# Last dense block of an attention and two-layer expert kernel: low parts on VectorE, a constant subtracted on ScalarE, the element chain on 1024 columns, splits one half-step sooner

## The chip, the cores and the metric

One core of one Trainium2 chip. The metric is the device time of one execution in microseconds; lower is better. A core has a matmul engine (TensorE, PE in the rows, with its weight loads as PEld), VectorE (DVE), ScalarE (ACT), GpSimd (POOL) and SyncE, whose queue (SPq) starts the transfers. Each engine takes its instructions in the order in which the program gives them and waits on semaphores for the others.

## What is computed

Three blocks follow one another on 2304 tokens (4 sequences of 576): attention with 8 heads, a layer of 8 experts of which each token uses one, and a last dense block. The change concerns the last block alone:

```python
def _moe2_ref(x, w_in, w_out):        # x 2304 x 512, w_in 512 x 2048, w_out 2048 x 512
    h = x @ w_in
    g = h * np.cos(h)
    return (g @ w_out).astype(np.float32)
```

All tensors are float32. The kernel multiplies in a reduced form of float32 (fp32r): it splits each operand in a high part (a copy into fp32r) and a low part (operand minus high part), and adds three products, high x high, high x low and low x high.

## The kernel before

Attention and experts take the first 546 us; the function `moe2` (line 1384) is the last block and takes the rest, together with transfers and splits that run ahead of it.

**Units.** The 2304 tokens are a first group of 256 (g = 0) and four groups of 512 (g = 1 to 4). The 2048 hidden features are 8 pieces q of 256. The weights of half of them fit, so there are two passes, w = 0 (q = 0 to 3) and w = 1 (q = 4 to 7). The order of the units (lines 1400 to 1406) is g = 0 with four q, then g = 1 to 4 for w = 0, then g = 1 to 4 for w = 1, then g = 0 again. For g > 0 a piece q is a pair of units, i = 0 and i = 1, each a half-step; for g = 0 it is one unit. That makes 72 units; a group of 512 tokens is eight of them, and the groups begin at t = 4, 12, 20, 28, 36, 44, 52, 60.

**Layer 1** (`layer1`, line 1444) forms h for a piece of 256 features and 512 tokens by Strassen's method in seven products of half size (`product`, line 1437): i = 0 computes four (24 matmuls of 256 columns), i = 1 three (18). The factors are sums of quarters of x (`sums`, line 1418: four 512-column operations per group) and of w_in (`Seven.sums`, line 1347), each split in high and low part: seven tiles X0 to X6 (line 1395, one buffer each, so that a group overwrites those of the one before) and seven blocks per q in a slot. `middle` (line 1470) adds the products up: for i = 0 a copy p on ScalarE and four sums of 256 columns on VectorE, which also give half of the second h; for i = 1 two sums (512 and 256 columns) that finish both h.

**The element chain** of a unit, on 128 x 512: `angles` (line 1490) computes k = h / 2 pi + MAGIC on ScalarE, which rounds to a whole number; `reduced` (line 1494) calls `reduce` (line 1325): subtract MAGIC from k, and two scalar_tensor_tensor that take the multiple of 2 pi off h, all on VectorE; `sines` (line 1498) does Sin and Square on ScalarE; `cosines` (line 1503) one scalar_tensor_tensor on VectorE that gives g = -h cos(h) / 2; `split_g` (line 1507) the high part on ScalarE and the low part on GpSimd.

**Layer 2** (`layer2`, line 1514) adds g times w_out into four accumulators in PSUM, 12 matmuls of 512 columns per unit; after a group's last unit `results` (line 1543) takes them out and stores them: in pass 0 as partial sums to the scratch tensor Y1, in pass 1 added to what `recall` (line 1538) has read back.

**The order** is the loop at line 1598. In iteration t: layer 1 of unit t, chain steps of earlier units, `middle` of t, `split_g`, the work that falls due (`later.step`), layer 2 of unit t - 5. The helper `lag` gives the units of a chain step: for g > 0 it is one iteration later than for g = 0. Work that falls due: at t - 3 of a group's first unit `fetch` reads its x into the two buffers xd (shared with results and recall, so a fetch waits until a group's results are stored), at t - 2 `sums` runs on GpSimd, and the x splits (`split_x`, line 1432: high part ScalarE, low part VectorE) come two at t - 2, two at t - 1 and three at t.

**Weights.** `build` (line 1570) puts the seven-product weights of a piece q into a slot: `Seven.parts` (line 1376) loads, then high parts on ScalarE, sums on GpSimd and low parts on the engine given. Pieces 1 to 3 are built in iterations 0 to 9, pieces 4 to 7 from t1 - 14 to t1 + 3, where t1 = 36. `split_out` (line 1564) does the w_out pieces 4 to 7 at t1 - 1, + 1, + 3, + 5: high part on ScalarE, low part on GpSimd (`Dense.split`, line 803).

## Time and profile before

| | us |
|---|---|
| median of three runs | 1031.33 |
| lowest and highest | 1028.74, 1035.77 |
| the profiled execution | 1032.09 |
| its span, first to last instruction | 1030.3 |

In that span TensorE is busy for 930.1 us, VectorE 856.7, ScalarE 575.6, GpSimd 378.0. The mean granted TensorE clock is 0.958 of full speed. Times in the rows are microseconds from the span's start, unless marked ns. A row of the timeline gives start, duration, engine, line, operation, and output <- inputs with their shape; an idle time before it and what ended that stand in brackets. Tiles go by the names in the program: x are the split factors of layer 1, xt their sums, xd what was read or is to be stored, k and r the chain's tiles, ph the PSUM tile of layer 1, py that of layer 2, s and w weights, xc and xo raw weights.

### The profile page before, as it was taken

What the parts mean: (1) busy time and instruction counts of PE and PEld (TensorE: products, weight loads), DVE (VectorE), ACT (ScalarE), POOL (GpSimd) and SP (SyncE); (2) the same over time, 40 slices, a digit from 0 to 9 for tenths busy, and PEclk for the clock granted to TensorE, in tenths of its full rate; (3) what the DMA queues carried; (4) which work ended last, traced back from release to release, by engine and by line L of the source; (5) the groups of instructions that cost most, each with busy time, mean ns of one, the idle gap of its engine ahead of it and who ended that gap; (6) DMA issues with size and microseconds to landing.
All of it is one profiled execution on the core that took longest, in us unless ns stands there. A gap on an engine that the chain in (4) does not pass through costs nothing.

```text
span 1030.3 us, 20277 instructions
## 1 busy us (share of the span) xinstructions
PE 930.1 (90%) x7529; PEld 778.7 (76%) x7530; DVE 856.7 (83%) x1661; ACT 575.6 (56%) x1146; POOL 378.0 (37%) x433
## 2 busy tenths in 40 slices
PE   8999999999989999999996797989795879798996
PEld 4566666666669899898996686878685668687995
DVE  8958888888765678977988898898999998979872
ACT  8867777777774433434445554555564554544551
POOL 0034545455560122233224352435256442424231
PEclk9989999999999999999999799989898999998999
DMA  7965355545374645477763110303031122211202
GB/s 218 292 214 161 128 186 178 194 149 168 113 248 148 202 161 178 119 256 261 262 206 108 42 62 1 102 1 103 1 124 52 68 65 64 76 62 65 83 1 86
DMA packets 69161, 134.12 MB, mean 130 GB/s; under 512 B 7048, under 2 KB 19100, under 8 KB 69052
## 3 DMA queue, kind: packets, MB, share of 16 engines
q1 hardware_dynamic: 68764, 132.57, 39.7%
q8 instruction: 61, 1.00, 0.4%
q14 instruction: 48, 0.39, 0.1%
q10 hardware_dynamic: 288, 0.16, 0.1%
HBM read 94.38 MB, written 38.32 MB: 129 GB/s over the span
## 4 chain that ended last, share of the span: by engine, by line
PE 42%; DVE 27%; issue 6%; DMA 3%; POOL 1%; ACT 1%; SPq 0%; DVEq 0%; POOLq 0%; ACTq 0%
PE py L1528 11%; PE ph L1441 8%; PE pl L861 7%; PE po L880 6%; DVE x L1435 5%; DVE g L1505 3%; DVE r L1328 3%; PE pa L602 3%; DVE k L1327 3%; PE ps_s L524 3%; DVE h L1476 2%; DVE u L1476 2%; PE Tp L560 1%; DVE w L811 1%; DMA Wo<-f32a 1%
## 5 line engine op out<-in xcount | busy, mean ns | idle before, releaser
L1511 POOL TENSOR_TENSOR gl<-g,gh 128x512 fp32r<-128x512 f32 x72 | 101.4, 1409 | 265.6 <-ACT gh L1510 255.1
L1528 PE MATMUL py<-w,gh 128*128 128x512 f32 x576 | 188.9, 410 | 3.7 <-DVE xd L1553 2.6
L1441 PE MATMUL ph<-x,s 128*128 128x256 f32 x840 | 122.0, 300 | 58.2 <-DVE x L1435 46.1
L1441 PEld LDWEIGHTS ph<-x,s 128*128 128x128 f32 x840 | 115.1, 205 | 67.1 <-DVE x L1435 51.1
L1322 ACT ACTIVATE k<-h,magic 128x512 f32<-128x512 f32 x64 | 46.0, 719 | 150.4 <-DVE h L1476 150.4
L1528 PEld LDWEIGHTS py<-w,gh 128*128 128x128 f32 x576 | 108.6, 198 | 26.2 <-DVE xd L1553 3.4
L861 PE MATMUL pl<-xh,w 128*128 128x288 f32 x512 | 118.2, 306 | 0.5 <-DVE hl L866 0.5
L1528 PE MATMUL py<-w,gl 128*128 128x512 f32 x288 | 117.2, 407 | 1.1 <-POOL gl L1511 1.1
L534 DVE CUSTOM_DVE_ANT_0 s<-ps_s,Bp 128x576 f32<-128x576 f32 x112 | 81.1, 755 | 40.7 <-PE ps_s L524 31.1
L545 ACT ACTIVATE e<-s,mn 128x576 f32<-128x576 f32 x144 | 110.3, 769 | 6.8 <-DVE mn L534 6.6
L880 PE MATMUL po<-hh,w 128*128 128x288 f32 x512 | 112.8, 297 | 0.2 <-DVE w L811 0.2
L720 POOL TENSOR_TENSOR f32a<-f32a,raw 128x256 f32<-128x256 f32 x64 | 48.2, 753 | 146.6 <-DVE raw L718 118.2
L861 PEld LDWEIGHTS pl<-xh,w 128*128 128x128 f32 x512 | 88.4, 194 | 5.4 <-issue 3.2
L524 PEld LDWEIGHTS ps_s<-HL 64*128 64x128 f32 x768 | 57.3, 189 | 39.8 <-DVE mn L534 20.9
L524 PE MATMUL ps_s<-HL 64*128 64x288 f32 x768 | 76.6, 316 | 11.4 <-DVE mn L534 9.9
L880 PEld LDWEIGHTS po<-hh,w 128*128 128x128 f32 x512 | 86.3, 190 | 0.4 <-DVE w L811 0.4
L865 ACT ACTIVATE hh<-pl 128x288 fp32r<-128x288 f32 x64 | 26.3, 411 | 97.3 <-PE pl L861 96.1
L602 PE MATMUL pa<-eT,V 128*64 128x320 f32 (+1 forms) x512 | 79.4, 420 | 0.0
L861 PE MATMUL pl<-xl,w 128*128 128x288 f32 x256 | 77.4, 302 | 1.7 <-DVE xl L835 1.7
L880 PE MATMUL po<-hl,w 128*128 128x288 f32 x256 | 75.9, 297 | 0.0
L571 ACT ACTIVATE eT<-Tp 128x512 f32<-128x512 f32 x80 | 46.1, 598 | 41.3 <-PE Tp L560 41.2
L1528 PEld LDWEIGHTS py<-w,gl 128*128 128x128 f32 x288 | 56.4, 196 | 15.8 <-POOL gl L1511 1.9
(258 smaller groups left out, 2176.8 us busy)
## 6 DMA issues: line engine op xcount, KB each, us to landing
Bp<-in_w SPq DMA_DIRECT2D x38, 512.0 KB, 6.0
Bd<-ev SPq DMA_DIRECT2D x36, 295.5 KB, 3.7
Rqk<-in_qk SPq DMA_DIRECT2D x16, 576.0 KB, 5.3
raw<-in_w_in SPq DMA_DIRECT2D x32, 256.0 KB, 4.0
raw<-in_w_out SPq DMA_DIRECT2D x32, 256.0 KB, 3.7
xd<-X SPq DMA_DIRECT2D x16, 512.0 KB, 4.2
Bp<-Bd SPq DMA_DIRECT2D x28, 288.0 KB, 5.9
X<-xT SPq DMA_DIRECT2D x7, 1152.0 KB, 5.4
```

Of the source, the lines that this page charges most:

```text
L524: nc.tensor.matmul(p[:, hf, :HF], w, y, start=(x == 0), stop=(x == 2))
L534: nc.vector.tensor_tensor_reduce(out=h2(s), in0=ps[:, :, :HF], in1=h2(bias(hp, i)), scale=-0.125, scalar=3e38, op0=ALU.add, op1=ALU.min, a ...
L545: nc.scalar.activation(out=e[:, par, :], in_=s, func=AF.Exp, bias=mn, scale=-1.0, accum_out=acc)
L571: nc.scalar.activation(out=dst, in_=Tp[qh], func=AF.Copy)
L602: nc.tensor.matmul(pa[64 * par:64 * par + 64, :W], d["V"][:, k, par, :], x, start=(k == 0), stop=(k == 4))
L720: self.tc.nc.gpsimd.tensor_tensor(out=af[:], in0=af[:], in1=low, op=ALU.add)
L861: nc.tensor.matmul(ps[:, :HF], w[:, c, :], x[:, c, :], start=(n == 0), stop=(n == 3 * NP_ - 1))
L880: nc.tensor.matmul(self.acc[d][:, :HF], w[:, ds_], x, start=(f == 0 and n == 0), stop=(f == self.FC - 1 and n == 2))
L1435: eng.tensor_tensor(out=X[k][:, 1], in0=src, in1=X[k][:, 0].bitcast(F32), op=ALU.subtract)
L1441: nc.tensor.matmul(out, W[:, l, a, c, :], x[:, m, c, :], start=(first and n == 0), stop=(last and n == 5))
L1511: nc.gpsimd.tensor_tensor(out=lo, in0=g, in1=hi.bitcast(F32), op=ALU.subtract)
L1528: nc.tensor.matmul(st["acc"][k], x[:, c], a, start=(first and n == 0), stop=(last and n == (2 if g else 5)))
```

## The change

The chain of a pair of units (g > 0) runs once on 1024 columns, in tiles that `wide` hands out: one tile for the pair, of which g = 0 units use a half each. `lag` now gives the second unit of a pair without the extra iteration, and the chain steps of that pair all run then. MAGIC is taken off k by a second ScalarE instruction with a bias tile `back`; `reduced` keeps the two scalar_tensor_tensor. The cosine writes r in place. The low part of g is computed on VectorE, `split_g` runs at a lag of two, layer 2 at t - 4, and the loop ends one iteration sooner. The low parts of the seven-product weights go to GpSimd; of the four w_out pieces 4 and 6 have their low parts on VectorE, 5 and 7 on GpSimd. The first group's x splits are due one iteration sooner for the first five. The buffers of p and u fall to one each; k has one of 1024 columns, h, r, gh and gl two.

```diff
@@ -1388,12 +1388,20 @@
     later = Later()
     with ExitStack() as ctx:
         pool = lambda name, bufs, **kw: ctx.enter_context(tc.tile_pool(name=name, bufs=bufs, reuse_waits="tile", **kw))
-        wp, xp, tp, gp, dp = pool("p3w", 1), pool("p3x", 1), pool("p3t", 3), pool("p3g", 3), pool("p3d", 2)
+        wp, xp, tp, gp, dp = pool("p3w", 1), pool("p3x", 1), pool("p3t", 1), pool("p3g", 2), pool("p3d", 2)
         ps_h, ps_o = pool("ps_h", 4, space=PSUM), pool("ps_y", 1, space=PSUM)
         slots = dense.slots + [dense.slot(wp, "s1"), dense.seven(dense.blocks[1]), dense.seven(dense.blocks[0]),
                                dense.slot(wp, "s4")]
         X = [xp.tile([128, 2, 2, XG], F32R, name=f"x{k}") for k in range(7)]
-        t512 = lambda name, bufs=3: tp.tile([128, TG], F32, name=name, bufs=bufs)
+        pairs = {}
+
+        def wide(t, name, bufs, pool=tp, dt=F32):
+            w, g, q, i = units[t]
+            if g or q % 2 == 0:
+                pairs[name] = pool.tile([128, 2 * TG], dt, name=name, bufs=bufs)
+            return pairs[name] if g else pairs[name][:, TG * (q % 2):TG * (q % 2) + TG]
+
+        t512 = lambda name: tp.tile([128, TG], F32, name=name, bufs=1)
         xd = lambda name="xd", bufs=2: dp.tile([128, 1024], F32, name=name, bufs=bufs)
         v = nc.vector
 
@@ -1475,25 +1483,29 @@
             near, far = slice(0, XG), slice(XG, TG)
             add = lambda out, a, b: v.tensor_tensor(out=out, in0=a, in1=b, op=ALU.add)
             if i == 0:
-                p, u = st["p"], st["u"] = t512("p", 2), t512("u", 2)
-                h1 = d[t + 1]["h"] = t512("h", 4)
+                p, u = st["p"], st["u"] = t512("p"), t512("u")
+                hh = d[t + 1]["h"] = wide(t, "h", 2)
+                h0, h1 = st["h"] = hh[:, 0:TG], hh[:, TG:2 * TG]
                 nc.scalar.activation(out=p, in_=A, func=AF.Copy)
                 add(u[:, near], C[:, near], p[:, near])
                 add(u[:, far], C[:, far], u[:, near])
                 add(h1[:, far], u[:, far], p[:, far])
                 add(p[:, far], u[:, near], p[:, far])
             else:
-                h0 = d[t - 1]["h"] = t512("h", 4)
+                h0, h1 = st["h"]
                 add(h0, A, st["p"])
-                add(d[t]["h"][:, near], C[:, near], st["u"][:, far])
+                add(h1[:, near], C[:, near], st["u"][:, far])
 
         def angles(t):
-            k = d[t]["k"] = t512("k", 2)
+            k = d[t]["k"] = wide(t, "k", 1)
             turns(nc, k, d[t]["h"], bias)
+            nc.scalar.activation(out=k, in_=k, func=AF.Identity, bias=back)
 
         def reduced(t):
-            r = d[t]["r"] = t512("r", 3)
-            reduce(nc, r, d[t]["k"], d[t]["h"])
+            r, k = wide(t, "r", 2), d[t]["k"]
+            d[t]["r"] = r
+            v.scalar_tensor_tensor(out=r, in0=k, scalar=-PI2A, in1=d[t]["h"], op0=ALU.mult, op1=ALU.add)
+            v.scalar_tensor_tensor(out=r, in0=k, scalar=-PI2B, in1=r, op0=ALU.mult, op1=ALU.add)
 
         def sines(t):
             r = d[t]["r"]
@@ -1501,15 +1513,17 @@
             nc.scalar.activation(out=r, in_=r, func=AF.Square)
 
         def cosines(t):
-            g = d[t]["g"] = t512("g", 2)
-            v.scalar_tensor_tensor(out=g, in0=d[t]["r"], scalar=0.5, in1=d[t]["h"], op0=ALU.subtract, op1=ALU.mult)
+            r = d[t]["r"]
+            v.scalar_tensor_tensor(out=r, in0=r, scalar=0.5, in1=d[t]["h"], op0=ALU.subtract, op1=ALU.mult)
 
         def split_g(t):
-            g = d[t]["g"]
-            hi, lo = gp.tile([128, TG], F32R, name="gh"), gp.tile([128, TG], F32R, name="gl")
+            g = d[t]["r"]
+            n = 2 if units[t][1] else 1
+            hi, lo = (wide(t, x, 2, gp, F32R) for x in ("gh", "gl"))
             nc.scalar.activation(out=hi, in_=g, func=AF.Copy)
-            nc.gpsimd.tensor_tensor(out=lo, in0=g, in1=hi.bitcast(F32), op=ALU.subtract)
-            d[t] = dict(hi=hi, lo=lo)
+            v.tensor_tensor(out=lo, in0=g, in1=hi.bitcast(F32), op=ALU.subtract)
+            for i in range(n):
+                d[t + 1 - n + i] = dict(zip(("hi", "lo"), (x[:, TG * i:TG * i + TG] for x in (hi, lo))))
 
         def layer2(t):
             w, g, q, i = units[t]
@@ -1563,7 +1577,7 @@
 
         def split_out(q):
             dense.w[1, q] = dense.w[1, q - 4]
-            dense.split(B, 1, q, None, nc.gpsimd)
+            dense.split(B, 1, q, None, nc.gpsimd if q % 2 else v)
             if q < 7:
                 load_out(q + 1)
 
@@ -1571,13 +1585,15 @@
             for dt, fn in seven.parts(q, slots[k], eng):
                 at(t + dt, fn)
 
-        warm = t512("p", 2)
+        warm = t512("p")
+        back = tp.tile([128, 1], F32, name="back")
+        nc.gpsimd.memset(back, -MAGIC)
         nc.scalar.activation(out=warm[0:1, 0:1], in_=bias[0:1, :], func=AF.Sin, scale=0.0)
         fetch(0, 1)
         for k, t in enumerate((0, 3, 5)):
-            build(t, k + 1, k + 1, v)
+            build(t, k + 1, k + 1, nc.gpsimd)
         at(0, lambda: sums(v))
-        for t, k in ((1, 0), (1, 3), (2, 4), (2, 5), (3, 1), (3, 2), (4, 6)):
+        for t, k in ((0, 0), (0, 3), (1, 4), (1, 5), (2, 1), (3, 2), (4, 6)):
             at(t, lambda k=k: split_x(k, v))
         for (w, g), t in start.items():
             if g and (w, g) != (0, 1):
@@ -1593,22 +1609,23 @@
         for q in range(4, 8):
             seven.corner[q] = tiles[q // 6].rearrange("p c t -> p (c t)")[:, 512 * (q % 2):512 * (q % 2) + 512].rearrange(
                 "p (l c f) -> p l c f", l=2, c=2)
-            build(t1 - 14 + (0, 7, 10, 13)[q - 4], q, (4, 0, 1, 2)[q - 4], v)
+            build(t1 - 14 + (0, 7, 10, 13)[q - 4], q, (4, 0, 1, 2)[q - 4], nc.gpsimd)
             at(t1 - 1 + 2 * (q - 4), lambda q=q: split_out(q))
-        for t in range(N + 5):
+        for t in range(N + 4):
             if t < N:
                 layer1(t)
-            lag = lambda n: [s for s in (t - n, t - n - 1) if 0 <= s < N and (s == t - n) == (units[s][1] == 0)]
+            lag = lambda n: [s for s in (t - n, t - n) if 0 <= s < N and units[s][1] == 0][:1] + [
+                s for s in (t - n,) if 0 <= s < N and units[s][3] == 1]
             for work, n in ((angles, 1), (sines, 2), (reduced, 1), (cosines, 2)):
                 for s in lag(n):
                     work(s)
             if t < N:
                 middle(t)
-            for s in lag(3):
+            for s in lag(2):
                 split_g(s)
             later.step()
-            if t >= 5:
-                layer2(t - 5)
+            if t >= 4:
+                layer2(t - 4)
 
 
 MAGIC = 12582912.0
```

## Rows read from the trace of the kernel before

**Rows 1.** Windows: stretch and length, busy us per engine (instructions), granted clock, DMA share, GB/s

```profile
557.90:566.86 8.96, 0.12 (x3) 0.03 (x1) 8.64 (x13) 6.10 (x12) 3.81 (x4) 0.72 0.03 13
566.86:619.78 52.92, 44.56 (x252) 39.65 (x253) 48.75 (x68) 28.89 (x49) 23.64 (x20) 0.89 0.16 50
619.78:670.32 50.54, 44.66 (x266) 39.35 (x264) 44.25 (x66) 25.88 (x45) 17.13 (x13) 0.97 0.15 53
670.32:720.04 49.72, 45.76 (x266) 40.24 (x264) 45.29 (x68) 27.43 (x48) 19.75 (x17) 0.93 0.17 54
720.04:772.00 51.96, 45.30 (x266) 39.96 (x264) 50.01 (x71) 29.16 (x53) 22.88 (x17) 0.93 0.20 62
772.00:834.00 62.00, 46.51 (x259) 39.51 (x260) 60.58 (x74) 30.55 (x52) 34.75 (x24) 0.89 0.20 68
834.00:886.19 52.19, 45.85 (x270) 40.31 (x269) 47.68 (x70) 27.22 (x48) 20.53 (x15) 0.97 0.20 65
886.19:936.50 50.31, 44.59 (x265) 39.37 (x264) 44.29 (x68) 24.77 (x43) 17.16 (x13) 0.97 0.18 62
936.50:985.45 48.95, 45.70 (x267) 40.46 (x266) 43.89 (x73) 24.17 (x42) 12.23 (x9) 0.93 0.19 63
```

**Rows 2.** Chain that ended last, 936 us to the end: start, us, what

```profile
953.85 2.84 PE ph L1441 x24
956.69 2.80 PE py L1528 x12
959.49 2.12 PE ph L1441 x18
...
1005.41 16.81 PE py L1528 x72
```

**Rows 3.** Waits, 560 us to the end: us in total, times, longest us

```profile
PE ph L1441 <- DVE x L1435: 46.1, 19, 9.3
```

**Rows 4.** Timeline of all engines around 881 us

```profile
881.32 1.36 POOL L1422 TENSOR_TENSOR xt<-xd,xt 128x512 f32<-128x512 f32 x1
881.45 1.79 DVE L1435 TENSOR_TENSOR x<-xd,x 128x512 fp32r<-128x512 f32 x1
```

**Rows 5.** Single operations by line or tile: shortest/median/longest ns, first and last start

```profile
L1435 DVE TENSOR_TENSOR x<-xt,x x32: 676/684/1789, 563.6 to 949.3; 128x512 fp32r<-128x512 f32 x32
...
L1476 DVE TENSOR_TENSOR h<-ph,p x32: 677/684/687, 581.7 to 983.1; 128x512 f32<-128x512 f32 x32
...
L1476 DVE TENSOR_TENSOR h<-u,p x32: 424/425/614, 577.5 to 978.9; 128x256 f32<-128x256 f32 x32
...
L1327 DVE TENSOR_SCALAR k<-k x72: 411/426/2642, 559.7 to 1006.2; 128x512 f32<-128x512 f32 x72
...
L811 POOL TENSOR_TENSOR w<-xo,w x4: 2382/2684/3384, 778.5 to 821.2; 128x1024 fp32r<-128x1024 f32 x4
...
L1350 POOL TENSOR_TENSOR xc<-xc x32: 720/942/1195, 538.0 to 799.2; 128x256 f32<-128x256 f32 x32
```

**Rows 6.** Groups by form, 700 to 1000 us: busy us, mean ns, idle before

```profile
L1322 ACT ACTIVATE k<-h,magic 128x512 f32<-128x512 f32 x45 | 32.4, 719 | 109.2 <-DVE h L1476 109.2
...
L1500 ACT ACTIVATE r<-r 128x512 f32<-128x512 f32 x47 | 29.1, 620 | 0.0
...
L809 ACT ACTIVATE w<-xo 128x1024 fp32r<-128x1024 f32 x4 | 4.2, 1046 | 0.0
...
L1374 DVE TENSOR_TENSOR w<-xc,w 128x1024 fp32r<-128x1024 f32 x1 | 1.2, 1218 | 0.0
```

**Rows 7.** Timeline of SyncE's queue, 868 to 900 us

```profile
871.17 1.57 SPq L1557 DMA_DIRECT2D out<-xd  x2
874.01 1.84 SPq L1415 DMA_DIRECT2D xd<-X  x2
```

**Rows 8.** Timelines of VectorE and of GpSimd, 795 to 800 us

```profile
797.55 1.11 DVE L1329 SCALAR_TENSOR_TENSOR r<-k,r 128x512 f32<-128x512 f32 x1
...
796.06 4.36 POOL L1350 TENSOR_TENSOR xc<-xc 128x256 f32<-128x256 f32 x4
```

## The prediction, made before the changed kernel was run

> **What bounds the kernel now.** I cut the last stage (the second dense block, from 557.9 us to the end) at the first matmul of each group of 512 tokens and read the windows of those stretches first [rows 1]. A group asks the same matmuls everywhere, yet takes 49.0 to 62.0 us. The chain of waits says what an undisturbed pair of half-steps costs TensorE: 2.84 + 2.80 + 2.12 + 2.80 = 10.56 us, so 42.2 for the four pairs of a group [rows 2]. Every group is 7 to 20 us above that floor, and in each window it is VectorE that is busy for 44 to 61 us. In the waits the largest that TensorE suffers there is for the low parts of x, 46.1 us in 19 waits [rows 3]: the transition from one group to the next, where X is overwritten in place.
>
> Why VectorE is late there is seen in a timeline [rows 4]: the x split takes 1.79 us while GpSimd runs its 512-column sums, where the same operation at best takes 0.68 [rows 5]. GpSimd's own operation ends first, then the split runs. Operations that read PSUM escape: the 512-column sum h from ph is 677 to 687 ns in all 32 cases [rows 5], while the tensor_scalar on k goes from 411 to 2642 ns [rows 5]. So work on GpSimd is paid for on VectorE, about 1.1 us for each 512-column operation that collides.
>
> **The change, part by part.** Durations for 1024 columns: a VectorE tensor_tensor of that size takes 1.22 us and a ScalarE copy 1.05, against 0.68 and 0.62 for 512 [rows 5, 6]. The trace shows no 1024-column scalar_tensor_tensor, Sin, Square or biased Identity. Above, they are bounded by two halves (1.37 on VectorE, 1.24 on ScalarE, 1.44 with bias); below by the 1.22 and 1.05. I take the lower ones, which are of the same size, and for the biased form 0.72 + 0.43 = 1.15, the 0.43 being 1.05 - 0.62 [rows 6].
>
> *Low parts of g from GpSimd to VectorE.* Per group, eight GpSimd operations go that could each block VectorE by 1.1 us (8.8 at most); four of 1.22 come onto VectorE. The subtraction leaves VectorE (8 of 0.41 at best), and two pairs of three-operand instructions become single ones (12 fewer starts: 24 of 0.68 become 12 of 1.22, less 1.7 us). VectorE's own load: -3.3 - 1.7 + 4.9, about zero. What goes is the blocking.
>
> *The chain as a loop.* A pair's turn needs its h, which stands on VectorE behind the cosine of the pair before. From turn to turn: 1.15 turn + 1.15 subtraction + 2 x 1.22 + 1.05 + 1.05 + 1.22 cosine + 1.1 for the two h (0.68 + 0.42) = 9.2, with 0.1 for handing over 9.3 us. The four sums of the next pair (0.42 each [rows 5]) lie beside Sin and Square, gl beside the next turn. TensorE's 10.56 covers the loop with 1.3 to spare, 5.2 in a group. Against this stand, per group: two x splits ahead of a cosine +0.65 (0.6 each from start to start, of which 0.55 lie in its wait for Square), two x high parts ahead of a turn +1.05, three x splits +1.3 (1.8 less 0.5), results (2 on each engine or 4 on VectorE, about 0.6 each, 1.1 of it in the shadow of the next turn) +1.2, together 4.2; and the four GpSimd sums, 4 x 1.1 x 0.8 (VectorE is waiting for something the rest of the time) = 3.5. 7.7 - 5.2 = 2.5 over the floor: 44.7, taken as 45.0 a group. With two halves in place of each wide instruction the loop is 2 x 1.44 + 2 x 1.37 + 2 x 1.24 + 1.37 + 1.1 + 0.1 = 10.7, no spare, and a group is 42.2 + 7.7 = 50, as now; without collisions it is 43.
>
> *Split one half-step sooner.* Layer 2 runs four half-steps behind layer 1 instead of five. The y stores, and the fetch of the next X that follows them on SP (871.2 then 874.0 [rows 7]), move some 5 us ahead of the layer-1 work that they serve. With gl gone, GpSimd has nothing queued before the sums, so most of them end before the x splits begin. That is why I let the stall shrink to 2.5. The queues passed: SP's order of stores, recall and fetch is kept; ScalarE's high part waits for its cosine with the turn of the next pair behind it, 1.05 that is inside the loop's shadow of the two h. The tail after the last layer-1 step is now 72 layer-2 matmuls in 16.81 us [rows 2], six half-steps; one less is 2.8. This one fills TensorE's idle time at the stage's start instead.
>
> *Weight lows to GpSimd.* Per q of the seven-product weights: 512 + 256 (+256) + 1024 columns; a 1024-column low takes 2.38 there at best against 1.22 [rows 5], the 256-column sums that were there already 0.72 at best [rows 5]. GpSimd's load per q: 4 x 0.95 [rows 5] + 1.3 [rows 4] + 2 x 0.75 + 2.4 = 9.0 us. The matmuls that need them come two to three half-steps (10 us or more) after the last low is queued, so GpSimd's 2.4 to 3.4 is covered; late, it would cost TensorE up to 3 a q. What they cost VectorE: a 256-column sum lengthens the colliding 512-column operation from 0.68 to 1.11, so 0.43 [rows 5, 8], a 512-column one 1.1, the 1024 about 2.2 (2.62 against 0.41 is the longest k [rows 5]). Per q 1.7 + 1.9 + 2.2 = 5.8; three q and two of the four w_out lows (2.2 each) fall into the fourth and fifth group: 22 x 0.6 = 13, plus 2.4 for the two lows that VectorE takes, plus 2 x 2.5 as above: 20 over a floor of 84.4, so 105 instead of 52.0 + 62.0. Bounds 92 (no collision) and 114 (nothing gained). The third group has q = 4 in it: 47.
>
> The Trainium skill (SBUF — State Buffer, Who interferes with whom) has the loser fully blocked for the whole instruction. The long GpSimd operations agree, the 256-column ones show 0.43 [rows 5, 8] and not their 0.72; by the rule four sums cost 1.2 us more per q, and the pair of groups would be 107. I go by the row.
>
> The Trainium skill (ScalarE: Activation LUTs, Rules for kernel authors) would leave an add on VectorE. At best VectorE's is 0.41 against 0.72 for the biased form on ScalarE [rows 5, 6]; by the rule the loop would be about 0.3 shorter per pair and a group up to 1.2 us faster without this edit. But that operation averages more than its best because it is one that collides, up to 2.6 us [rows 5].
>
> *Start.* From 557.9 to 619.8 it is 9.0 + 52.9 = 61.9 us, 19.5 above a floor. VectorE loses the k operations and three sets of lows, GpSimd gains these. Between 0 and 8 gained; I take 4, mostly the layer-2 half-step that fits into the wait.
>
> **Sum.** Four ordinary groups (50.5, 52.2, 50.3, 49.0 = 202.0) to 180: -22.0. Third group 49.7 to 47: -2.7. Fourth and fifth 114.0 to 105: -9.0. Start -4.0, tail -2.8. Together -40.5. The profiled execution has 1032.1 us (span 1030.3): 991.6. It stands 0.8 above the median of 1031.3, so 991.
>
> **Rivals.**
> *TensorE-bound throughout.* For it: once past a transition, groups run at the floor today [rows 2]. Against: X is still overwritten in place. Groups 43, third 43, pair 88, start 55, tail 2.8: -30 - 7 - 26 - 7 - 3 = -73, 959.
> *Little left of it.* Wide instructions cost near two halves, or the builds collide fully: groups 48, third 49.7, pair 114, start -2, tail -2.8: -10 - 5 = -15, 1016. For it: VectorE's own load does not fall. Against: the 1.22 and 1.05 of the 1024-column rows.
> *Slower: the chain one pair deep.* Today's two half-steps interleave; now a pair goes through two ScalarE and VectorE turns with single k, p and u tiles. If the next pair's four sums, which wait for layer 1 and stand ahead of the cosine, fall into the loop rather than beside Sin and Square, it is 9.3 + 1.75 = 11.05 a pair, a group 44.2 + 7.7 = 51.9, on eight groups 1.7 more each against 50.2, less the tail: +11, and with the pair of groups no better 1043. It decides from a loop of 10.7, where a group equals today's. Against: GpSimd no longer blocks those sums.
>
> **Chances.** Forecast 0.63 (977 to 1006), TensorE-bound 0.15, little left 0.17, slower 0.05. Range 972 to 1013: it leaves out most of the first rival and the upper third of the second and third. About 1% (10 us) is what a measurement tells here. Faster by more: 0.63 + 0.15 + 0.12 = 0.90; within: 0.05 + 0.01 = 0.06; slower: 0.04.
>
> **What would show it.** Right: ordinary groups of 44 to 46 us between first layer-1 matmuls; TensorE's wait for x splits under 20 us in total; x splits near 0.68; first GpSimd sum of a transition at least 3 us ahead of the first x split; 60 matmuls in the last chain piece. Wrong: wide scalar_tensor_tensor above 1.3 us, VectorE's cosine waiting for GpSimd in ordinary groups, TensorE waiting for gl or for weight lows on GpSimd, or a loop from turn to turn above 10.7.

## The result and the profile after

The changed kernel takes 997.12 us (median of four runs, 996.5 to 998.38) against 1031.46 for the kernel before beside it; the ratio is 0.967, with a 95% interval of 0.963 to 0.970. The change gains 34 us; 40 were forecast (991, range 972 to 1013). The profiled execution of after has a span of 994.7 us, 35.6 less than before, and a mean clock of 0.973 of full speed against 0.958.

The windows of after, cut at the same matmuls as [rows 1] (stretch and length, busy us of PE, PEld, DVE, ACT and POOL with instructions, granted clock, DMA share, GB/s):

```profile
555.28:618.53 63.25, 45.98 (x265) 40.41 (x265) 54.82 (x62) 38.95 (x55) 33.97 (x25) 0.89 0.14 44
618.53:664.44 45.91, 42.73 (x265) 38.09 (x264) 38.59 (x50) 28.38 (x33) 11.24 (x8) 1.00 0.17 58
664.44:712.46 48.02, 44.22 (x265) 39.61 (x264) 38.78 (x49) 30.57 (x37) 16.85 (x11) 0.96 0.17 56
712.46:760.88 48.42, 44.65 (x265) 39.41 (x264) 41.29 (x51) 31.49 (x40) 21.05 (x15) 0.96 0.19 66
760.88:815.87 54.99, 46.59 (x265) 40.82 (x264) 43.99 (x50) 35.08 (x42) 27.50 (x18) 0.94 0.24 77
815.87:865.72 49.85, 45.35 (x266) 40.32 (x265) 43.72 (x58) 29.31 (x34) 7.74 (x6) 0.93 0.22 74
865.72:909.68 43.96, 42.21 (x265) 38.01 (x264) 38.96 (x52) 28.13 (x33) 7.53 (x4) 1.00 0.23 73
909.68:953.31 43.63, 42.37 (x267) 38.16 (x266) 35.69 (x50) 27.82 (x30) 0.00 (x0) 1.00 0.19 61
953.31:994.70 41.39, 33.27 (x193) 29.07 (x191) 19.69 (x26) 15.86 (x24) 0.00 (x0) 0.93 0.16 53
```

Read the second column against [rows 1]. The first row is the start of the stage, two rows of before (61.9 us); then come the seven other groups and the tail. Two groups now stand 1.8 and 1.4 us above the floor of 42.2, at a granted clock of 1.00. Term by term:

| stretch | before | forecast | after |
|---|---|---|---|
| start | 61.9 | 57.9 | 63.25 |
| four ordinary groups | 202.0 | 180 | 183.35 (45.91, 49.85, 43.96, 43.63) |
| third group | 49.7 | 47 | 48.0 |
| fourth and fifth (builds) | 114.0 | 105 | 103.4 |
| last stretch | 44.85 | 42.05 | 41.4 |
| the part that was not changed | 557.9 | 557.9 | 555.3 |

The last row is not put down to the edits: in the twelve profiles of after and its variants this part ended anywhere between 555.3 and 559.4 us, and the profile of after has the shortest. So 2.6 of the 35.6 us by which its span is shorter are not the change's. Each stretch is read from one profile, and stretches of the same code differ by a few us between profiles: the group of 49.85 us takes 47.1 in a variant below that changes the first three builds alone.

The waits of after, 560 us to the end (engine line waited for: us in total, times, longest):

```profile
PE ph L1449 <- DVE x L1443: 19.4, 15, 2.8
...
PE ph L1449 <- DVE r L1517: 12.5, 2, 10.8
...
PE ph L1449 <- ACT x L1442: 9.8, 6, 2.4
```

The wait for the low parts of x, 46.1 us in 19 waits before [rows 3], is 19.4 in 15, the longest 2.8 instead of 9.3. A new one has come: 9.8 us for the high parts of x on ScalarE, which has no row among TensorE's waits before. The 12.5 us for r is the start: TensorE waits there for the first cosine. Forms of the wide instructions (busy us, mean ns, idle before), then the shortest, median and longest of single operations:

```profile
L1322 ACT ACTIVATE k<-h,magic 128x1024 f32<-128x1024 f32 x32 | 36.5, 1142 | 4.8 <-DVE h L1484 4.6
...
L1502 ACT ACTIVATE k<-k,back 128x1024 f32<-128x1024 f32 x32 | 36.9, 1152 | 1.0
```

```profile
L1507 DVE SCALAR_TENSOR_TENSOR r<-k,h x32: 1216/1226/2311, 585.8 to 953.4; 128x1024 f32<-128x1024 f32 x32
...
L1524 DVE TENSOR_TENSOR gl<-r,gh x40: 677/1225/2372, 566.6 to 981.7; 128x1024 fp32r<-128x1024 f32 x32, 128x512 fp32r<-128x512 f32 x8
...
L1443 DVE TENSOR_TENSOR x<-xt,x x32: 677/684/1780, 558.2 to 917.3; 128x512 fp32r<-128x512 f32 x32
```

The prices taken at the lower bound were right as medians: 1.22 us for the three-operand instruction and for gl, 1.15 for the biased form. The mean of the first three-operand instruction is 1.36 (43.6 us for 32), since some still run beside GpSimd. ScalarE's turn, whose idle time in [rows 6] was 109 us behind h, now waits 4.6 for it. That alone does not say that the chain is shorter: the high part of g now stands just ahead of the turn, and ScalarE waits 81.9 us there for the cosine. The last piece of the chain of waits is `py x60` in 13.62 us, for x72 in 16.81 [rows 2]: one half-step less.

### The profile page after: what moved, and what is told of

The parts are those of the page before. It is cut to its first block, busy times and chain, and to the rows that moved or that the text cites. A ratio compares the mean times of both kernels' runs of the same rounds, so it can differ in the third digit from the quotient of the medians.

```text
span 994.7 us, 19932 instructions
## 1 busy us (share of the span) xinstructions
PE 915.4 (92%) x7529; PEld 769.8 (77%) x7530; DVE 798.7 (80%) x1510; ACT 602.0 (61%) x1058; POOL 321.0 (32%) x385
## 3 DMA queue, kind: packets, MB, share of 16 engines
q1 hardware_dynamic: 68764, 132.57, 41.4%
## 4 chain that ended last, share of the span: by engine, by line
PE 38%; DVE 19%; ACT 8%; issue 8%; DMA 5%; POOL 2%; SPq 1%; POOLq 0%; DVEq 0%; ACTq 0%
PE py L1542 9%; PE ph L1449 7%; PE pl L861 6%; PE po L880 5%; PE pa L602 3%; DVE r L1507 3%; PE ps_s L524 3%; DVE r L1517 2%; ACT k L1502 2%; DVE x L1443 2%; ACT k L1322 2%; DVE w L811 2%; PE Tp L560 1%; DMA Wo<-f32a 1%; DVE h L1484 1%
## 5 line engine op out<-in xcount | busy, mean ns | idle before, releaser
L1542 PE MATMUL py<-w,gh 128*128 128x512 f32 x576 | 183.2, 400 | 1.7 <-ACT xd L1565 1.0
L1449 PE MATMUL ph<-x,s 128*128 128x256 f32 x840 | 118.8, 295 | 42.3 <-DVE x L1443 19.4
L1449 PEld LDWEIGHTS ph<-x,s 128*128 128x128 f32 x840 | 112.0, 200 | 51.1 <-DVE x L1443 23.2
L1542 PEld LDWEIGHTS py<-w,gh 128*128 128x128 f32 x576 | 106.5, 194 | 21.4 <-ACT xd L1565 1.3
L861 PE MATMUL pl<-xh,w 128*128 128x288 f32 x512 | 116.1, 302 | 0.2 <-DVE hl L866 0.2
L1542 PE MATMUL py<-w,gl 128*128 128x512 f32 x288 | 114.4, 397 | 0.0
L1523 ACT ACTIVATE gh<-r 128x1024 fp32r<-128x1024 f32 (+1 forms) x40 | 39.0, 975 | 81.9 <-DVE r L1517 81.9
L524 PE MATMUL ps_s<-HL 64*128 64x288 f32 x768 | 76.8, 317 | 11.3 <-DVE mn L534 9.4
L865 ACT ACTIVATE hh<-pl 128x288 fp32r<-128x288 f32 x64 | 26.2, 410 | 94.2 <-PE pl L861 91.6
L1507 DVE SCALAR_TENSOR_TENSOR r<-k,h 128x1024 f32<-128x1024 f32 x32 | 43.6, 1363 | 33.5 <-ACT k L1502 33.5
L1542 PEld LDWEIGHTS py<-w,gl 128*128 128x128 f32 x288 | 55.6, 193 | 12.5 <-DVE gl L1524 0.3
```

The costliest lines, as they stand in the source:

```text
L524: nc.tensor.matmul(p[:, hf, :HF], w, y, start=(x == 0), stop=(x == 2))
L861: nc.tensor.matmul(ps[:, :HF], w[:, c, :], x[:, c, :], start=(n == 0), stop=(n == 3 * NP_ - 1))
L1449: nc.tensor.matmul(out, W[:, l, a, c, :], x[:, m, c, :], start=(first and n == 0), stop=(last and n == 5))
L1507: v.scalar_tensor_tensor(out=r, in0=k, scalar=-PI2A, in1=d[t]["h"], op0=ALU.mult, op1=ALU.add)
L1523: nc.scalar.activation(out=hi, in_=g, func=AF.Copy)
L1542: nc.tensor.matmul(st["acc"][k], x[:, c], a, start=(first and n == 0), stop=(last and n == (2 if g else 5)))
```

## The experiments

The median of the kernel before was 1030.06, 1029.26, 1030.73 and 1031.77 us beside the four sets of runs; ratios are to it.

**The low part of g back on GpSimd.**

```diff
-            v.tensor_tensor(out=lo, in0=g, in1=hi.bitcast(F32), op=ALU.subtract)
+            nc.gpsimd.tensor_tensor(out=lo, in0=g, in1=hi.bitcast(F32), op=ALU.subtract)
```

> The changed kernel with the low part of g computed on GpSimd again (1024 columns at once), all else as changed. Theory A, that the gain is VectorE no longer standing still while GpSimd works: four GpSimd operations of about 2.4 us per group come back, each able to hold VectorE for up to 2.2 us, so ordinary groups go from 44-46 back to 47-50 us and the time to 1010-1030. Rival B, that the gain comes from wider and fewer instructions and the earlier split: VectorE even loses 4.9 us of work per group, so the time stays at 990-1002.

Measured: 1019.43 us, ratio 0.990 (0.987 to 0.992), 22 slower than after. TensorE waits only 1.9 us for gl itself. It waits 27.5 us in 17 for low parts of x, and 10.9 us in 2 for weight low parts that stand behind gl on GpSimd. The x splits on VectorE (by form, 560 us to the end; first this kernel, then after) show what GpSimd's work does beside them:

```profile
L1443 DVE TENSOR_TENSOR x<-xt,x 128x512 fp32r<-128x512 f32 x32 | 33.5, 1067 | 5.0 <-ACT x L1442 5.0
```

```profile
L1443 DVE TENSOR_TENSOR x<-xt,x 128x512 fp32r<-128x512 f32 x31 | 23.8, 788 | 0.0
```

A mean of 1067 ns for 788, and VectorE, with the 48 us of gl gone (42.0 for the wide form, 6.0 for the other), is busy only 24 us less (774.7 for 798.7). So the engine matters through what else lies beside and behind it, and hardly as a wait for the result. By stretches the four ordinary groups take 184.6 us, in after 183.4; theory A had them at 47 to 50 each. What is lost lies in the start (74.5 for 63.25) and in the fourth and fifth group (111.3 for 103.4), where GpSimd also has the weight lows, and 4 us of this profile in the part that was not changed. The start:

```profile
559.41:633.91 74.50, 50.97 (x266) 45.52 (x266) 50.55 (x59) 41.98 (x60) 45.02 (x32) 0.79 0.12 38
```

**That part alone, in the kernel before** (512 columns; the cosine in place makes room).

```diff
-            r = d[t]["r"] = t512("r", 3)
+            r = d[t]["r"] = t512("r", 4)
...
-            g = d[t]["g"] = t512("g", 2)
+            g = d[t]["g"] = d[t]["r"]
...
-            nc.gpsimd.tensor_tensor(out=lo, in0=g, in1=hi.bitcast(F32), op=ALU.subtract)
+            v.tensor_tensor(out=lo, in0=g, in1=hi.bitcast(F32), op=ALU.subtract)
```

> The kernel before with one part of the change alone: the low part of g on VectorE in 512 columns (the cosine writes r in place and r has four buffers, which gives the same tile room). Theory A: most of the gain is there without wide instructions, 1000-1015. Rival B: VectorE gets 8 x 0.6 = 5 us more work per group on the engine that is busiest, and loses about as much blocking: 1022-1040, no gain.

Measured: 1012.09 us, ratio 0.982 (0.978 to 0.985). This part alone gives 18 of the 33 us; the wait for low parts of x falls from 46.1 to 31.3 us in 10 waits, and 8.3 us for gl come in. Here the gain does lie in the ordinary groups: 185.4 us for 202.0.

**The half-step undone** (split of g at a lag of three, layer 2 at t - 5).

```diff
-        for t in range(N + 4):
+        for t in range(N + 5):
...
-            for s in lag(2):
+            for s in lag(3):
...
-            if t >= 4:
-                layer2(t - 4)
+            if t >= 5:
+                layer2(t - 5)
```

> The changed kernel with the split of g and layer 2 one half-step later again (split at a lag of three, layer 2 five half-steps behind layer 1). Theory A: the tail is 2.8 us longer (72 matmuls in the last piece of the chain), and the y stores and the fetch behind them come 5 us later, so that GpSimd's sums meet the x splits again, 1 to 2 us per transition: 1003-1012. Rival: only the tail counts, 999.5-1001.

Measured: 1026.29 us, ratio 0.996 (0.994 to 0.998). Nearly all of the gain is gone, 29 us, more than any theory allowed. Its waits, 560 us to the end, and its timeline at a group's turn:

```profile
ACT k L1322 <- DVE h L1484: 126.2, 31, 6.7
...
PE ph L1449 <- DVE x L1443: 38.3, 16, 5.8
```

```profile
891.10 1.22 DVE L1524 TENSOR_TENSOR gl<-r,gh 128x1024 fp32r<-128x1024 f32 x1
892.23 1.28 DVE L1443 TENSOR_TENSOR x<-xd,x 128x512 fp32r<-128x512 f32 x2
892.97 3.99 PE L1449 MATMUL ph<-x,s 128*128 128x256 f32 x17 [3.30 <-DVE x L1443]
...
894.04 1.21 DVE L1517 SCALAR_TENSOR_TENSOR r<-r,h 128x1024 f32<-128x1024 f32 x1
```

With the split an iteration later, gl lands in the half-step that already has two three-operand instructions and four sums, ahead of the x splits and the cosine; those come later by its 1.22 us, h with them, and ScalarE's turn waits 126 us for h, as in the kernel before. The 17 matmuls behind the stall take 3.99 us, against 2.3 in other places: TensorE runs them at the lower clock level (granted clock 0.50 from 892.97 to 896.96). How long the chain's loop has become is seen from one turn on ScalarE to the next, first here, then in the kernel with the x splits sooner (below):

```profile
897.46 1.15 ACT L1322 ACTIVATE k<-h,magic 128x1024 f32<-128x1024 f32 x1 [5.48 <-DVE h L1484]
908.74 1.15 ACT L1322 ACTIVATE k<-h,magic 128x1024 f32<-128x1024 f32 x1 [3.15 <-DVE h L1484]
```

```profile
909.68 1.14 ACT L1322 ACTIVATE k<-h,magic 128x1024 f32<-128x1024 f32 x1
918.97 1.14 ACT L1322 ACTIVATE k<-h,magic 128x1024 f32<-128x1024 f32 x1
```

It is 11.3 us with the split late, more than TensorE's 10.56 for a pair [rows 2], and 9.3 where the split stands as changed and nothing else holds the chain. So with the late split the chain sets the pace of nearly every pair, and the four ordinary groups take 200.8 us, as in the kernel before (202.0).

**Layer 2 alone at t - 5**, the split as changed.

```diff
-        for t in range(N + 4):
+        for t in range(N + 5):
...
-            if t >= 4:
-                layer2(t - 4)
+            if t >= 5:
+                layer2(t - 5)
```

> The changed kernel with layer 2 five half-steps behind layer 1, but the split of g where the change has it. It parts the two halves of the half-step, after the run that undid both cost 29 us. Theory E, that what costs there is the place of the low part of g on VectorE (behind the four sums of the next pair and ahead of the x splits and the cosine, so inside the loop from turn to turn): here the place is the changed one, so only the tail (2.8 us) and the later fetch count, 999-1005. Rival F, that the lag of layer 2 costs by itself (later stores, later fetch, GpSimd's sums on the x splits): 1015-1028.

Measured: 1013.89 us, ratio 0.986 (0.984 to 0.989): between the two, nearer to the second. So, undone in this order, some 17 of the 29 us belong to layer 2's place and 12 to the split's. The first GpSimd sum of the same turn in this kernel and, in the second fence, in after, and the first x split:

```profile
864.03 1.30 POOL L1430 TENSOR_TENSOR xt<-xd 128x512 f32<-128x512 f32 x1 [39.87 <-DMA xd<-X]
...
869.21 1.77 DVE L1443 TENSOR_TENSOR x<-xd,x 128x512 fp32r<-128x512 f32 x1
```

```profile
851.94 1.30 POOL L1430 TENSOR_TENSOR xt<-xd 128x512 f32<-128x512 f32 x1 [34.63 <-DMA xd<-X]
...
861.68 0.68 DVE L1443 TENSOR_TENSOR x<-xd,x 128x512 fp32r<-128x512 f32 x1
```

The sums wait for X to be fetched, and the fetch for the results of the group before to leave its buffers. One half-step later, the lead over the first split falls from 9.7 to 5.2 us, the fourth sum still runs when the split starts, and the split takes 1.77 instead of 0.68 us. Over all seven turns the sums lead by 6.1 to 12.4 us in after, by 3.8 to 6.5 here and by 1.7 to 3.4 in the kernel before.

**The x splits of later groups one half-step sooner**, which the change did for the first group alone.

```diff
-                for dt, k in ((-2, 0), (-2, 3), (-1, 4), (-1, 5), (0, 1), (0, 2), (0, 6)):
+                for dt, k in ((-2, 0), (-2, 3), (-2, 4), (-2, 5), (-1, 1), (-1, 2), (-1, 6)):
```

> The changed kernel with the x splits of a group due one half-step sooner: X0, X3, X4, X5 all at t - 2 and X1, X2, X6 at t - 1, each still behind its last reader in layer 1. Theory C, that what is left over the floor in ordinary groups is TensorE waiting at a transition for x splits that stand behind the chain on VectorE and behind the high part of g on ScalarE (19.4 + 9.8 us of waits and the lower granted clock after them): the waits fall below 8 us in total and the time to 975-986. Rival D, that VectorE is short of time as a whole: the wait moves to the cosine or to layer 2 and the time stays within 4 us of 997.

Measured: 991.33 us, ratio 0.962 (0.960 to 0.965), 6 better than after and between the theories. TensorE's wait for low parts of x is 7.9 us in 5; 6.4 us in 4 for the high part of g come in their place, since the x high parts now stand ahead of it on ScalarE, and one of 4.1 for ScalarE's eviction of a group's results. By stretches theory C holds where it looked: the ordinary groups take 174.2 us for 183.4 and the third 46.0 for 48.0. But the fourth and fifth group take 108.9 for 103.4, with the longest of the new waits, and so the time stays above theory C's.

**The subtraction back on VectorE.**

```diff
-            nc.scalar.activation(out=k, in_=k, func=AF.Identity, bias=back)
...
+            v.tensor_scalar(out=k, in0=k, scalar1=-MAGIC, scalar2=None, op0=ALU.add)
```

> The changed kernel with MAGIC taken off k by VectorE again, 1024 columns in one tensor_scalar (about 0.68 us if free, one half of 1.15 less than ScalarE's 1.15), all else as changed. Theory A: with GpSimd mostly silent the operation is rarely blocked and the loop from turn to turn gets 0.45 us shorter per pair, while VectorE gets 2.7 us more per group: 993-999. Rival, that VectorE's time counts at the transitions and in the groups with builds: 1000-1008.

Measured: 1003.59 us, ratio 0.975 (0.973 to 0.977), 6.5 slower than after. On VectorE the 1024-column form averages 0.96 us, against 1.15 on ScalarE (by form, 560 us to the end):

```profile
L1506 DVE TENSOR_SCALAR k<-k 128x1024 f32<-128x1024 f32 x32 | 30.7, 958 | 4.9 <-ACT k L1322 4.8
```

ScalarE is slower at it by 0.2 us, and the kernel is still faster with it there: the likely reason is that VectorE is rid of 30.7 us. By stretches the start is 3.6 us longer (66.8) and the ordinary groups 1.7 together (185.0), as far as one profile tells, whose part that was not changed is longer by 2.8 as well. The Trainium skill (ScalarE: Activation LUTs, Rules for kernel authors) would leave an add on VectorE; the prediction worked out up to 1.2 us a group in favour of that rule, and the run decides against it.

**Low parts of the weights on VectorE**: all of them, or those of the first three builds.

```diff
-            build(t, k + 1, k + 1, nc.gpsimd)
+            build(t, k + 1, k + 1, v)
...
-            build(t1 - 14 + (0, 7, 10, 13)[q - 4], q, (4, 0, 1, 2)[q - 4], nc.gpsimd)
+            build(t1 - 14 + (0, 7, 10, 13)[q - 4], q, (4, 0, 1, 2)[q - 4], v)
```

> The changed kernel with all low parts of the seven-product weights on VectorE again (q = 1 to 7). Theory A by the prediction's prices: VectorE gets 2.4 us per q, and GpSimd's collisions of up to 4.1 us per q (0.6 of them felt, 2.5) go, so nothing much moves: 993-1001, the pair of groups at 101-106 as now (103.4). Rival, that the move to GpSimd is what made room in the pair of groups: pair at 108-112, 1003-1010.

> The changed kernel with the low parts of q = 1 to 3 alone on VectorE, q = 4 to 7 on GpSimd. It asks why the start gained nothing (63.2 us from the first layer-1 unit's end to the second group, 58 predicted). Theory G, that GpSimd's lows hold VectorE while TensorE waits for the first cosines and x splits (x splits of 2.88 for two and 2.48 for one): the start falls by 2-4 us, 993-995. Rival H, that VectorE is simply full there and gets 7 us of lows more: the start grows by 2-5, 999-1002.

Measured: 995.84 (992.75 to 996.66) and 995.06 us (992.49 to 998.11), both ratio 0.967 with intervals of 0.964 to 0.970. Neither can be told from after. In the first the fourth and fifth group take 104.0 us together, 103.4 in after. In both the start grows, which rival H had expected of the second, to 67.1 and 65.8 us from 63.25, and the group behind it makes up for that (41.9 and 42.4 for 45.9). In the second the start's first wait falls from 10.8 to 9.5 us, but the third build, now behind the chain on VectorE, is waited for:

```profile
612.55 3.55 PE L1449 MATMUL ph<-x,w 128*128 128x256 f32 x16 [4.84 <-DVE w L1374]
```

**Layer 2 at t - 5 with the x splits sooner**, to see whether layer 2's place is paid for only by the x splits.

```diff
-                for dt, k in ((-2, 0), (-2, 3), (-1, 4), (-1, 5), (0, 1), (0, 2), (0, 6)):
+                for dt, k in ((-2, 0), (-2, 3), (-2, 4), (-2, 5), (-1, 1), (-1, 2), (-1, 6)):
...
-        for t in range(N + 4):
+        for t in range(N + 5):
...
-                layer2(t - 4)
+                layer2(t - 5)
```

> The kernel of a_x_sooner with layer 2 at t-5 in place of t-4 (the split of g stays at lag 2). In the changed kernel the same edit of layer 2 cost some 17 us (a_l2_only), of which the last chain piece (72 matmuls for 60, 2.8 us) accounts for a sixth. Theory G: the rest is paid at the group turns alone, where ScalarE, held for a buffer of the high part, brings the high parts of the sums late and TensorE stalls and then runs at the lower clock; with the x splits a half-step sooner the turns no longer stall, so the edit costs little beside the tail, 990-997 us. Theory H: the buffers of g, free a half-step later, hold the chain in every half-step: 1002-1010 us, with high part waiting for TensorE above 15 us in total.

Measured: 1013.07 us, ratio 0.982 (0.979 to 0.985), 22 more than without the edit. By time it is theory H, by mechanism it is neither. The high part's waits for TensorE are 15.6 us in 9 (8.1 and 7.5), but TensorE does not wait for the high part at all. It waits for the place of its results (waits, then the timeline of one such place):

```profile
PE py L1542 <- DVE xd L1567: 10.5, 4, 3.2
PE py L1542 <- DVE xd L1563: 8.3, 4, 2.3
```

```profile
902.00 1.23 DVE L1508 SCALAR_TENSOR_TENSOR r<-k,r 128x1024 f32<-128x1024 f32 x1
...
904.52 0.42 DVE L1484 TENSOR_TENSOR p<-u,p 128x256 f32<-128x256 f32 x1
...
904.86 2.48 DVE L1563 SCALAR_TENSOR_TENSOR xd<-py,xd 128x512 f32<-128x512 f32 x4
...
905.69 0.70 PE L1542 MATMUL py<-w,gh 128*128 128x512 f32 x2 [2.27 <-DVE xd L1563]
```

A group's last layer 2 falls in the other kind of half-step: its evictions stand behind two three-operand instructions and four sums of the even half-step, and the next group's first layer 2 needs the accumulators at once. 18.8 us in eight places, and 2.8 for the longer tail, make 21.6. That this meets the 22 is no proof: other waits moved too (6.4 for the high part of g and most of the 4.1 for ScalarE's eviction went, 3.6 more for low parts of x and 4.2 for h came).

**The same with layer 2 and its results given out right behind layer 1.**

```diff
             if t < N:
                 layer1(t)
+            if t >= 5:
+                layer2(t - 5)
...
-            if t >= 5:
-                layer2(t - 5)
```

> The kernel of x_l2 (x splits a half-step sooner, layer 2 at t-5) with layer 2 and the results of a group given out right behind layer 1, ahead of the chain, the four sums and the splits of the same half-step. In x_l2 TensorE waited 18.8 us in eight places for the evictions of a group's results on VectorE, which stood behind two instructions of the chain and the four sums of an even half-step. Theory K: that order is what the half-step of layer 2 costs there; with the evictions ahead of them this wait falls below 6 us and the time to 992-1000 us. Theory L: VectorE, now waiting for layer 2 at the head of its queue, gives the sums and the chain later by the same 2 to 3 us at each of eight group ends, and the time stays at 1008-1018 us.

Measured: 1007.8 us, ratio 0.976 (0.973 to 0.979). Both theories are half right. The wait for the evictions is gone, but VectorE now waits 17.2 us at the head of its queue for layer 2 (11.2 and 6.0; 6.9 in the kernel above), and TensorE's wait for low parts of x goes from 11.5 to 28.6 us. So the order causes the 18.8 us, but mending it in this half-step gave back only 5 of the 22: what the evictions no longer wait for, VectorE then does. How much of the rest each of its waits costs stays open.

**What beats both: two builds' low parts on VectorE, then those of w_out too**, on the kernel with x splits sooner.

```diff
-            build(t, k + 1, k + 1, nc.gpsimd)
+            build(t, k + 1, k + 1, v if k < 2 else nc.gpsimd)
```

```diff
-            dense.split(B, 1, q, None, nc.gpsimd if q % 2 else v)
+            dense.split(B, 1, q, None, v)
```

> The kernel of a_x_sooner with the low parts of the first two builds of the stretch (q 1 and 2) on VectorE as before the change, the third on GpSimd. Theory I: at the start GpSimd's 2.4 us low parts stand ahead of the sums, so that the first x splits come late; with two of them at 1.2 us on VectorE the start loses some 2 to 3 us of its stalls, and the wait for the third build that a_start_dve showed (4.84 us) does not come: 986-990 us. Rival: what the start gains is waited for later, as in a_start_dve: 990-993 us.

> The kernel of x_q12 with all low parts of the output weights on VectorE as well (the change put two of four on GpSimd). Theory J: in the first group after the builds, GpSimd's low parts of 2.5 us stand ahead of the four sums; without them this group comes down by 1 to 3 us, to 985-989 us. Rival: VectorE, which has two low parts of 1.2 us more there, brings the low parts of g later by as much and TensorE waits for those, 988-993 us.

Measured: 990.77 us (988.07 to 994.75), ratio 0.963 (0.959 to 0.966), and 985.71 us (984.2 to 987.94), ratio 0.957 (0.954 to 0.960). The first can't be told from the kernel it starts from by its times, though its profile has a shorter start. The second is the fastest of the study, 11 us under after and 45 under the kernel before beside it. Windows of the start and of the fifth group, for x splits sooner alone, then with two builds on VectorE, then with w_out as well:

```profile
556.54:619.58 63.04, 47.83 (x264) 42.45 (x265) 54.66 (x63) 39.82 (x57) 33.90 (x25) 0.84 0.14 43
756.32:817.46 61.14, 49.33 (x265) 41.84 (x264) 48.22 (x54) 34.43 (x42) 30.70 (x20) 0.89 0.22 69
```

```profile
555.73:615.44 59.71, 47.18 (x264) 42.09 (x265) 50.60 (x67) 39.94 (x57) 26.22 (x19) 0.86 0.15 45
752.51:813.87 61.36, 50.06 (x266) 41.99 (x264) 48.59 (x54) 34.73 (x43) 30.76 (x20) 0.89 0.21 69
```

```profile
556.10:615.73 59.63, 46.95 (x264) 41.67 (x265) 50.61 (x67) 40.59 (x58) 26.07 (x19) 0.86 0.16 48
753.17:809.33 56.16, 46.98 (x266) 40.37 (x264) 49.35 (x54) 34.92 (x43) 26.37 (x18) 0.94 0.23 75
```

Two sets of weight lows on VectorE shorten the start by 3.3 us: GpSimd's 33.9 us there fall to 26.2 and VectorE, which does them, is busy for 50.6 instead of 54.7. The lows of w_out gain 5.2 in the fifth group and not, as theory J had it, in the group behind it, which takes 44.7 without this edit and 45.5 with it. All four times of the second kernel lie below all four of the first. Of the 5.2, matmuls that take 46.98 us for 50.06 at a higher granted clock make 3.1 and shorter waits 2.1: the wait of 4.1 for ScalarE's eviction is gone, and the longest one for the high part of g grows from 2.3 to 4.8. Why ScalarE comes sooner there was not separated.

## Why the prediction was right, and where its terms were off

**What bounds it, and by which mechanism: right for the kernel before, and only in part for the changed one.** The loss sat at the turns of the groups, in the low parts of x, and it came from GpSimd's work beside VectorE's: taking the low part of g off GpSimd alone gives 18 us there, and the ordinary groups of its profile are shorter by 16.6. In the changed kernel, giving it back costs 22, but hardly any of it in the ordinary groups (184.6 for 183.4), where the prediction had put more than half of its gain. So their gain has more than one sufficient cause, and "what goes is the blocking" is not shown to be the one that acts in the changed kernel. Besides, an x split of a sum needs the sum's result: whether a turn was late through VectorE being held or through the sums coming late was not separated. The rival of TensorE bound throughout (959) is seen in two groups only, 43.96 and 43.63.

**Ordinary groups, 183.3 for 180.** Three lie within 1.4 us of 45. The fourth, 49.85, was counted as ordinary and is not. The timeline of after at its turn:

```profile
807.50 2.51 POOL L811 TENSOR_TENSOR w<-xo,w 128x1024 fp32r<-128x1024 f32 x1 [14.40 <-ACT w L809]
...
815.86 1.45 POOL L1430 TENSOR_TENSOR xt<-xd,xt 128x512 f32<-128x512 f32 x1
...
816.12 1.75 DVE L1443 TENSOR_TENSOR x<-xd,x 128x512 fp32r<-128x512 f32 x1
...
817.92 1.57 PE L1449 MATMUL ph<-x,s 128*128 128x256 f32 x11 [1.77 <-DVE x L1443]
```

A w_out low part stands on GpSimd ahead of the four sums, the last sum still runs when the x split starts (1.75 us for 0.68), and TensorE stalls; 7 us later twelve matmuls of layer 2 take 4.23 us (granted clock 0.62) where 2.8 is usual [rows 2]. The prediction charged these lows to VectorE's time in the group before; their place in GpSimd's queue was not counted. With the x splits a half-step sooner the same turn waits 0.3 us for x and 1.5 for g, and the group takes 45.0.

**Fourth and fifth group, 103.4 for 105.** Right in sum, but the edit that it priced there, the weight lows on GpSimd, makes no difference that can be measured (995.84 and 997.12; the two groups 104.0 and 103.4). 13 of the 105 were for what GpSimd's lows do to VectorE, so that this number was met is luck in part.

**The start was wrong: +1.3 for -4.** The step that failed is "VectorE loses the k operations and three sets of lows, GpSimd gains these", with its gain between 0 and 8. No loss was allowed. VectorE's busy time in the start is 54.8 us, 57.4 before (8.64 + 48.75), so little was taken off; GpSimd's went from 27.5 to 34.0. The loss sits in the first wait: TensorE waits for the first cosine 10.8 us, where the same stretch before is 8.96 [rows 1]; the 52.45 us behind that are 0.5 shorter than before. Timelines of after, then of the kernel with two builds' low parts back on VectorE, show why:

```profile
560.62 2.84 POOL L1374 TENSOR_TENSOR s<-xc,s 128x512 fp32r<-128x512 f32 x2
...
561.13 2.88 DVE L1443 TENSOR_TENSOR x<-xt,x 128x512 fp32r<-128x512 f32 x2
...
566.08 2.90 PE L1449 MATMUL ph<-x,s 128*128 128x256 f32 x12 [10.80 <-DVE r L1517]
```

```profile
561.31 1.28 DVE L1443 TENSOR_TENSOR x<-xt,x 128x512 fp32r<-128x512 f32 x2
...
564.66 2.90 PE L1449 MATMUL ph<-x,s 128*128 128x256 f32 x12 [8.93 <-DVE r L1517]
```

The change put four x splits ahead of the first cosine where two stood, and the last two meet GpSimd's low parts of the weights: they end 0.55 us after those (563.46, 564.01) and take 2.88 us where they take 1.28 alone. The Trainium skill (SBUF — State Buffer, Who interferes with whom) calls the ports that VectorE and GpSimd share an exclusive lock and, for VectorE's 2-port modes, has the loser blocked for the whole instruction; these splits, which read two operands, agree with it at 2.88 us for 1.28. With the low parts of two builds back on VectorE the start is 59.7 and 59.6 us in two profiles, 2.2 under before, about half of the 4. Undoing the edit for all three does not help: the start is then 65.8, with the third build's wait in it. The earlier x splits were not run by themselves.

**The half-step was undersized.** The prediction priced it at 2.8 for the tail, and put what it does for the sums into the 2.5 us that a turn's stall was to shrink to. It named the way (the fetch of X comes sooner, so the sums end before the splits) and the runs show it: 9.7 us of lead at the turn shown and 5.2 without. In after the last sum ends before the first split in six of seven turns, in the kernel before in none. But 29 us hang on it, since it also decides in which kind of half-step gl and the results' evictions stand on VectorE. No term of the sum held that, and the terms don't add up: the low part of g (22), the half-step (29) and the subtraction (6.5) make 57 of 34. The parts overlap: in the ordinary groups the move of gl can be missing and the gain stays (184.6), or be all there is and bring it (185.4), and without the half-step the rest brings nothing (200.8). That a sum without these terms came within 6 us is luck in part, for it was built from a group's floor and stall and not from the edits.

**The slower rival** had its point at the right place. It feared that VectorE's work would fall into the chain's loop. In the changed kernel it does not: TensorE hardly waits for g (0.3 us), and with the x splits sooner, where turns come as close as the chain allows, its loop is 9.3 us, as the prediction added it up. With the split an iteration later it is 11.3, above the 10.7 from which the rival decides, and the gain is gone.

**The forecast's own signs.** TensorE waits 19.4 us for low parts of x, just under the 20 set; with the 9.8 for high parts it is 29, of which 4.2 fall in the start. The median x split is 0.684 us, the first sum comes 6 us or more ahead of the split, the last piece has 60 matmuls. Of the signs against it, the wide three-operand instruction is under 1.3 us by its median and over by its mean, the wait for gl is 0.3 us on a weight load, and there is none for weight lows.

## What to carry to other kernels

Where two engines of a kernel disturb each other, a move is priced by what its work meets on the other engine, not by its own length: 1.15 us on ScalarE beat 0.96 on VectorE, and 1.22 us on VectorE beat its place on GpSimd by 22 us. When a software pipeline is shifted by a step, list for both kinds of half-step what each in-order queue then holds, evictions and splits included; here that order was worth more than the latency saved (29 us against 2.8). Undo the parts singly before adding their gains: they summed to 57 where 34 was to be had. And look by stretches where a part's price falls: the 22 us fell mostly where GpSimd had other work, not in the groups for which the move was meant.

## What was not expected of the hardware

The price of a stall on TensorE can go on after it. In the kernel with the half-step undone, a wait of 3.30 us was followed by 17 matmuls in 3.99 us, where 17 after a wait of 1.75 us took 2.30 in after. The length of the one wait does not decide it: in after itself 17 matmuls behind a wait of 1.82 us took 3.81 (granted clock 0.55) and 17 behind one of 1.81 took 2.29 (1.00). The two levels are 1.2 and 2.4 GHz. So a group's excess over the floor is the sum of its stalls and of matmuls at the lower level behind them. In the group of 49.85 us, with a granted clock of 0.93, the waits are 4.5 us (1.77, 1.77 and 0.96), and the matmuls take 45.35 for the 42.2 of the floor, 3.15 more; in the groups of 43.96 and 43.63, at 1.00, they take 42.21 and 42.37.
